# Masking the scores of both half-heads with one VectorE instruction over two PSUM banks

## The chip, the cores and the metric

The kernel runs on one core of one Trainium2 chip. The metric is the device time of one execution in microseconds (us), taken on that core; lower is better. Three runs of the kernel before lie between 1209.99 and 1215.49 us, with a median of 1213.58 us.

## The reference, cut to what matters

A linear attention with a decay per channel feeds two mixtures of experts. The change lies in the attention alone.

```python
# attention: 4 batches x 8 heads, 768 steps, 48 channels
for t in range(S):
    state = alpha[:, :, t, :, None] * state + einsum('bhd,bhe->bhde', k[:, :, t], v[:, :, t])
    y[:, :, t] = einsum('bhd,bhde->bhe', q[:, :, t], state)
x = y.transpose(0, 2, 1, 3).reshape(3072, 384)
# mixture 1: each row goes to the best of 8 experts, out = gate * (relu(x @ w1[e]) @ w2[e])
# mixture 2: out = sum over 4 experts of p[:, e] * (relu(x @ w1[e]) @ w2[e])
```

## The kernel before, in words

The 3072 rows are cut into 24 units of 128 steps, six for each batch. Eight heads are held as four pairs, and the two heads of a pair lie on partitions 0 to 47 and 64 to 111 of the same tiles: these are the two halves, `h` = 0 and 1.

One pass of the loop at L819 works on several units at once, in an order written out by hand (the schedule is manual, so each engine runs its instructions in program order):

- `prep1` (VectorE, two scans per piece, L434 and L446) forms the running products of the decay for a coming group of three units; `prep2` (GpSimd, L459 and L460) multiplies them into the queries and keys.
- `S1(u)` multiplies keys with queries into scores. Eight matmuls (L480), in the order pair 0 half 0, pair 0 half 1, pair 1 half 0 and so on, write two PSUM tiles `A0` and `A1` of one bank (512 fp32 columns) each, one for each half. Then two VectorE instructions (L485), 512 columns each, multiply the tiles with the causal mask `tri` (128 columns, repeated four times) into the SBUF tile `At`. The rest of `S1` transposes the keys (`kn`, L492).
- `S3(u-2)` transposes the finished outputs of an earlier unit (`fin`, L558); `S2(u-1)` multiplies the masked scores of the unit before with the values (`y`, L516), adds the part of the state (L525) and forms the update of the state (`U`, L537), which VectorE adds at L547 to L550.

The matmuls of L480 appear in the trace as two passes each, so 16 for a unit. The masks of a unit thus stand in VectorE's queue between the scans of `prep1` and the state update, and the next unit's score matmuls may overwrite a bank only after its mask has been read.

The pool `psA` (two banks, tag "A") hands its banks out in turn. It also serves what comes after the attention: `early_rows` and `early_g1` (tiles `ext` and `eh`, the first 224 rows of the first expert, L686 to L711), the transposes `xt0` and the tiles `h` of the first expert (L159, L160). At the second expert the pools are closed (L247) and others take the eight banks. From there on come the experts: matmuls L135 to L137, L233 to L235 and L301 to L303, with a ReLU split by ScalarE (L126) and VectorE (L127).

Of the kernel before, what the change touches and what calls it, by code (L numbers as in the profile page):

```python
# [7 lines left out]
F32 = mybir.dt.float32  # L8
# [5 lines left out]
ALU = mybir.AluOpType  # L14
AX = mybir.AxisListType
PSUM = bass.MemoryType.PSUM

B, H, S, D = 4, 8, 768, 48
# [20 lines left out]
@with_exitstack  # L39
def tile_main(ctx: ExitStack, tc: tile.TileContext, a: dict, out: bass.AP):  # L40
    nc = tc.nc

    const = ctx.enter_context(tc.tile_pool(name="const", bufs=1))
    small = ctx.enter_context(tc.tile_pool(name="small", bufs=2))
    dram = ctx.enter_context(tc.tile_pool(name="dram", bufs=1, space=bass.MemoryType.DRAM))

    xs = dram.tile([E1 * NR, DM], F32, name="xs")
    info_d = dram.tile([NT, 8], F32, name="info_d")


    units = [(0, e, f) for e in range(E1) for f in range(NFB)]
    units += [(1, e, f) for e in range(E2) for f in range(NFB)]
    wraw, wtile, ids = {}, {}, {}
    w_loaded, w_split = [0], [0]

    def load_w(n):
        while w_loaded[0] < min(n, len(units)):
            u = w_loaded[0]
            t = wst.tile([128, 2 * DM], F32, tag="wraw", name="wraw")
            src = a["wu"][u]  # L60
            if NFB <= u < E1 * NFB:
                e = a["wu"][0:E1 * NFB].rearrange("(e f) r c -> e f r c", f=NFB)
                src = e[bass.ds(ids[u // NFB], 1), u % NFB].rearrange("o r c -> (o r) c")
            nc.sync.dma_start(out=t, in_=src)
            wraw[u] = t
            w_loaded[0] += 1

    def split_w(n):
        while w_split[0] < min(n, len(units)):
            u = w_split[0]  # L70
            load_w(u + 1)
            r = wraw.pop(u)
            t = wun.tile([128, 2, 2 * DM], F32R, tag="wu", name="wu")
            nc.scalar.activation(out=t[:, 0], in_=r, func=AF.Copy)  # L74
            nc.gpsimd.tensor_tensor(out=t[:, 1], in0=r, in1=t[:, 0].bitcast(F32), op=ALU.subtract)  # L75
            wtile[u] = t
            w_split[0] += 1

    with tc.manual_schedule():
        ti = const.tile([128, 2, 128], F32, name="ti")  # L80
        ident = ti[:, 1]
        inf = const.tile([128, 24, 8], F32, name="inf")
        keep = {
            "ident": ident,
            "ti": ti,
            "ordi": const.tile([128, 8], I32, name="ordi"),
            "offi": const.tile([128, 8], I32, name="offi"),
            "posi": const.tile([128, 24], I32, name="posi"),
            "inf": inf,
            "flag": const.tile([1, 1], I32, name="flag"),  # L90
            "ft": const.tile([128, 3], F32, name="ft"),
            "ones": const.tile([128, 8], F32, name="ones"),
        }
        with ExitStack() as fast:
            wun = fast.enter_context(tc.tile_pool(name="wun", bufs=10))
            wst = fast.enter_context(tc.tile_pool(name="wst", bufs=3))
            banks = fast.enter_context(ExitStack())
            ps = (banks.enter_context(tc.tile_pool(name="psA", bufs=2, space=PSUM)),
                  banks.enter_context(tc.tile_pool(name="ps1", bufs=1, space=PSUM)))
            scat = attention_and_routing(tc, a, small, keep, xs, info_d, wst, wtile, load_w, split_w, *ps)  # L100
            experts(fast, tc, a, keep, small, xs, info_d, scat, wtile, ids, load_w, split_w, out, banks, *ps)

    bad = nc.values_load(keep["flag"][0:1, 0:1], min_val=0, max_val=1000)
    with tc.If(bad > 0):
        general(tc, a, ident, out)


def order(tc, ins, names, why):
# [230 lines left out]
def attention_and_routing(tc, a, small, keep, xs, info_d, wst, wtile, load_w, split_w, psA, ps1):  # L339
    nc = tc.nc  # L340
# [4 lines left out]
    with ExitStack() as ctx:  # L345
# [14 lines left out]
        tri = keep["ti"][:, 0]  # L360
# [112 lines left out]
        def S1(u):  # L473
            g, cl = divmod(u, 3)
            At = wk.tile([128, 2, 4, 128], F32, tag="At", name="At")
            ps = [psA.tile([128, 4, 128], F32, tag="A", name=f"A{h}") for h in range(2)]
            for p in range(4):
                kt, qq = (x[g, p // 2][:, 2 * cl + p % 2, :] for x in (kts, qqs))
                for h in range(2):
                    nc.tensor.matmul(  # L480
                        ps[h][:, p, :], lhsT=kt[64 * h:64 * h + D], rhs=qq[64 * h:64 * h + D],
                        start=(p == 0), stop=True, skip_group_check=True,
                    )
            for h in range(2):
                nc.vector.tensor_tensor(  # L485
                    out=At[:, h], in0=ps[h], in1=tri.unsqueeze(1).to_broadcast([128, 4, 128]), op=ALU.mult
                )
            Ats[u] = At
            if u % 6 < 5:
                pk = ps1.tile([128, 4, R], F32, tag="kn", name="kn")  # L490
                for p in range(4):
                    nc.tensor.matmul(  # L492
                        pk[:, p, :], lhsT=kts[g, p // 2][:, 2 * cl + p % 2, :], rhs=ident[0:R, 0:R],
                        is_transpose=True, start=(p == 0), stop=True, skip_group_check=True,
                    )
                kn = wk.tile([128, 4, R], F32, tag="kn", name="kn_s")
                nc.scalar.activation(out=kn, in_=pk, func=AF.Copy)
                kns[u] = kn
# [303 lines left out]
        prep1(0, 0, 1, 3)  # L802
        prep2(0, 0, nc.vector, nc.gpsimd, 1, 3)
        S1(0)
        prep1(0, 1, 1, 3)
        prep2(0, 1, nc.vector, nc.gpsimd, 1, 3)
# [12 lines left out]
        for i in range(NU + 5):  # L819
# [26 lines left out]
            if 0 < i < NU:  # L846
                S1(i)
# [77 lines left out]
        def dot(out, t, x):  # L925
# [32 lines left out]
            out=pv, in0=ohb, in1=off.unsqueeze(1).to_broadcast([128, NU, 8]), op=ALU.mult  # L958
# [341 lines left out]
```

## Time and profile before

| | |
|---|---|
| three runs, median (lowest to highest) | 1213.58 us (1209.99 to 1215.49) |
| profiled execution, its own time | 1213.84 us |
| its span, first to last instruction | 1212.1 us |
| TensorE matmul busy | 1178.3 us, 97% of the span |
| VectorE busy | 393.9 us, 33% |
| the mask instructions (L485) | 48 of 676 ns, 30.4 us busy |
| score matmul passes (L480) | 384 in the attention, up to 146 us |
| mean granted TensorE clock | 0.987 of full speed |

The profile lists, for one execution, what each engine did and what it waited for. TensorE's busy share is high all the way through, and VectorE's is high in the first tenth of the span alone, so the share over the whole span says little about a stage: the stretch that holds the changed instructions is the attention, the first 164 us, and it has to be read by itself.

### The profile page before, as it was taken

Reading aid. Unit: us, or ns where it says so; the run is one execution under the profiler, and the core shown is the slowest. Engines: PE = TensorE matmul, PEld = TensorE weight load, DVE = VectorE, ACT = ScalarE, POOL = GpSimd, SP = SyncE. Lnnn points to the kernel's source line nnn. Section 1 sums busy time; section 2 is a strip of 40 time slices with the busy share of each in tenths; the row PEclk is TensorE's granted clock in tenths of the full one; section 3 lists DMA queues with packets and bytes.
Section 4 is the critical chain, followed back from the end, with each engine's and each line's share of the span. In section 5 each row is a group of like instructions: output and inputs, shape, how many; then the busy total and the mean of one; then the engine's idle time right before and its main releaser. Section 6 shows DMA issues by size and latency. Waiting matters only on the chain.

```text
span 1212.1 us, 17429 instructions
## 1 busy us (share of the span) xinstructions
PE 1178.3 (97%) x7219; PEld 1080.6 (89%) x7219; DVE 393.9 (33%) x823; ACT 326.6 (27%) x640; POOL 307.1 (25%) x221
## 2 busy tenths in 40 slices
PE   5999999999999999999999999999999999999996
PEld 4888889999999999999999999999999999999996
DVE  8999653222222222222221222222222212222221
ACT  2466524444444211111311111221111131111111
POOL 3558724776676200000400000220000030111111
PEclk9999979999999999999999999999999999999998
DMA  9995235554434200000300000120000010000000
GB/s 229 275 284 184 93 114 157 151 146 136 141 118 120 67 1 1 1 1 1 92 14 1 1 1 1 40 66 1 1 1 1 1 40 1 27 27 27 27 27 29
DMA packets 30032, 79.98 MB, mean 66 GB/s; under 512 B 7352, under 2 KB 11064, under 8 KB 28376
## 3 DMA queue, kind: packets, MB, share of 16 engines
q1 hardware_dynamic: 26104, 69.25, 19.7%
q0 software_dynamic: 3840, 9.54, 2.2%
q8 instruction: 58, 0.95, 0.3%
q14 instruction: 30, 0.25, 0.1%
HBM read 65.21 MB, written 13.57 MB: 65 GB/s over the span
## 4 chain that ended last, share of the span: by engine, by line
PE 86%; DVE 5%; issue 3%; POOL 0%; ACT 0%; DVEq 0%; POOLq 0%; ACTq 0%
PE h L135 14%; PE h L137 13%; PE h L136 13%; PE p L303 11%; PE p L302 11%; PE p L301 11%; PE o L234 3%; PE o L235 3%; PE o L233 3%; DVE bf L446 1%; DVE At L485 1%; PE fin L558 1%; PE y L516 1%; DVE G L434 1%; PE A L480 1%
## 5 line engine op out<-in xcount | busy, mean ns | idle before, releaser
L127 DVE SCALAR_TENSOR_TENSOR hl<-h,hh 128x512 fp32r<-128x512 f32 (+9 forms) x264 | 169.9, 644 | 733.4 <-ACT hh L126 719.0
L126 ACT ACTIVATE hh<-h 128x512 fp32r<-128x512 f32 (+9 forms) x264 | 148.3, 562 | 726.2 <-PE h L137 724.5
L75 POOL TENSOR_TENSOR wu<-wraw,wu 128x768 fp32r<-128x768 f32 x96 | 176.5, 1842 | 650.4 <-ACT wu L74 650.4
L303 PE MATMUL p<-wu,hl 128*128 128x384 f32 x768 | 258.8, 337 | 0.0
L302 PE MATMUL p<-wu,hh 128*128 128x384 f32 x768 | 258.2, 336 | 0.0
L301 PE MATMUL p<-wu,hh 128*128 128x384 f32 x768 | 258.0, 336 | 0.0
L135 PE MATMUL h<-x,wu 128*128 128x512 f32 (+1 forms) x600 | 233.0, 388 | 0.0
L137 PE MATMUL h<-x,wu 128*128 128x512 f32 (+1 forms) x600 | 230.6, 384 | 0.0
L136 PE MATMUL h<-x,wu 128*128 128x512 f32 (+1 forms) x600 | 227.9, 380 | 0.0
L302 PEld LDWEIGHTS p<-wu,hh 128*128 128x128 f32 x768 | 144.3, 188 | 7.4
L301 PEld LDWEIGHTS p<-wu,hh 128*128 128x128 f32 x768 | 144.4, 188 | 7.1
L303 PEld LDWEIGHTS p<-wu,hl 128*128 128x128 f32 x768 | 144.3, 188 | 0.0
L137 PEld LDWEIGHTS h<-x,wu 128*128 128x128 f32 x600 | 112.6, 188 | 26.6
L136 PEld LDWEIGHTS h<-x,wu 128*128 128x128 f32 x600 | 112.8, 188 | 16.1
L135 PEld LDWEIGHTS h<-x,wu 128*128 128x128 f32 x600 | 112.8, 188 | 14.5
L74 ACT ACTIVATE wu<-wraw 128x768 fp32r<-128x768 f32 x96 | 80.3, 840 | 44.2 <-PE p L303 34.1
L314 POOL DMA_INDIRECT out_dram<-acc,toki x24 | 23.4, 975 | 183.3 <-DVE acc L310 178.5
L135 PE MATMUL h<-xh,wu 128*128 128x224 f32 (+7 forms) x192 | 67.4, 351 | 0.3 <-DVE xl L198 0.3
L234 PE MATMUL o<-hl,wu 128*128 128x224 f32 (+7 forms) x192 | 65.6, 342 | 0.1
L233 PE MATMUL o<-hh,wu 128*128 128x224 f32 (+7 forms) x192 | 65.6, 342 | 0.0
L137 PE MATMUL h<-xl,wu 128*128 128x224 f32 (+7 forms) x192 | 65.5, 341 | 0.0
L136 PE MATMUL h<-xh,wu 128*128 128x224 f32 (+7 forms) x192 | 65.5, 341 | 0.0
(164 smaller groups left out, 1089.1 us busy)
## 6 DMA issues: line engine op xcount, KB each, us to landing
wraw<-in_wu_dram SPq DMA_DIRECT2D x96, 384.0 KB
tin<-in_aqk_dram SPq DMA_DIRECT2D x14, 1011.1 KB
xw<-xs SPq DMA_DIRECT2D x7, 672.0 KB
v<-in_v_dram SPq DMA_DIRECT2D x8, 576.0 KB
xs<-pre SPq DMA_DIRECT2D x8, 480.0 KB
tin<-in_aqk_dram SPq DMA_DIRECT2D x2, 448.0 KB
tin<-in_aqk_dram SPq DMA_DIRECT2D x2, 225.8 KB
tin<-in_aqk_dram SPq DMA_DIRECT2D x2, 224.0 KB
```

The source lines that it names most:

```text
L74: nc.scalar.activation(out=t[:, 0], in_=r, func=AF.Copy)
L75: nc.gpsimd.tensor_tensor(out=t[:, 1], in0=r, in1=t[:, 0].bitcast(F32), op=ALU.subtract)
L126: nc.scalar.activation(out=hh[:, 0:n], in_=ps, func=AF.Relu)
L127: nc.vector.scalar_tensor_tensor(out=hl[:, 0:n], in0=ps, scalar=0.0, in1=hh[:, 0:n].bitcast(F32), op0=ALU.max, op1=ALU.subtract)
L135: nc.tensor.matmul(ps, lhsT=w[:, 0, ks], rhs=xh(k), start=(k == 0), stop=False)
L136: nc.tensor.matmul(ps, lhsT=w[:, 1, ks], rhs=xh(k), start=False, stop=False)
L137: nc.tensor.matmul(ps, lhsT=w[:, 0, ks], rhs=xl(k), start=False, stop=(k == KD - 1))
L233: nc.tensor.matmul(o, lhsT=w[:, 0, ds], rhs=hh[:, 0:n], start=(f == 0), stop=False)
L234: nc.tensor.matmul(o, lhsT=w[:, 0, ds], rhs=hl[:, 0:n], start=False, stop=False)
L301: nc.tensor.matmul(o, lhsT=hh[:, js], rhs=w[:, 0, DM:2 * DM], start=(f == 0), stop=False)
L302: nc.tensor.matmul(o, lhsT=hh[:, js], rhs=w[:, 1, DM:2 * DM], start=False, stop=False)
L303: nc.tensor.matmul(o, lhsT=hl[:, js], rhs=w[:, 0, DM:2 * DM], start=False, stop=(f == NFB - 1))
```

## The change

The two score tiles of a unit become one tile of two banks, `[128, 2, 512]`, which is allocated once for the whole run by a small class `Banks`. The score matmuls write slices of it; one VectorE instruction of 1024 columns, with the mask repeated eight times, reads both banks and writes the whole of `At`. All other users of `psA` call `Banks.tile`, which hands out the two banks of the same tile in turn.

```diff
-            ps = (banks.enter_context(tc.tile_pool(name="psA", bufs=2, space=PSUM)),
+            ps = (Banks(banks.enter_context(tc.tile_pool(name="psA", bufs=1, space=PSUM))),
                   banks.enter_context(tc.tile_pool(name="ps1", bufs=1, space=PSUM)))
...
+class Banks:
+    def __init__(self, pool):
+        self.both = pool.tile([128, 2, 512], F32, name="A")
+        self.n = 0
+
+    def tile(self, shape, *_, **__):
+        self.n += 1
+        return self.both[0:shape[0], self.n % 2, 0:shape[1]]
...
         def S1(u):
-            ps = [psA.tile([128, 4, 128], F32, tag="A", name=f"A{h}") for h in range(2)]
+            ps = psA.both.rearrange("p h (a c) -> p h a c", a=4)
             for p in range(4):
                 kt, qq = (x[g, p // 2][:, 2 * cl + p % 2, :] for x in (kts, qqs))
                 for h in range(2):
                     nc.tensor.matmul(
-                        ps[h][:, p, :], lhsT=kt[64 * h:64 * h + D], rhs=qq[64 * h:64 * h + D],
+                        ps[:, h, p, :], lhsT=kt[64 * h:64 * h + D], rhs=qq[64 * h:64 * h + D],
                         start=(p == 0), stop=True, skip_group_check=True,
                     )
-            for h in range(2):
-                nc.vector.tensor_tensor(
-                    out=At[:, h], in0=ps[h], in1=tri.unsqueeze(1).to_broadcast([128, 4, 128]), op=ALU.mult
-                )
+            nc.vector.tensor_tensor(
+                out=At.rearrange("p h a c -> p (h a) c"), in0=ps.rearrange("p h a c -> p (h a) c"),
+                in1=tri.unsqueeze(1).to_broadcast([128, 8, 128]), op=ALU.mult,
+            )
```

## Rows read from the trace of the kernel before

**Rows 1.** The page's chain that ended last: shares by engine, then by line.
```profile
PE 86%; DVE 5%; issue 3%; POOL 0%; ACT 0%; DVEq 0%; POOLq 0%; ACTq 0%
```
**Rows 2.** Busy time by stretch: length, PE, PEld, DVE, ACT, POOL; PEclk, DMA, GB/s.
```profile
20.00:113.00 93.00, 88.28 (x1117) 77.14 (x1113) 85.11 (x198) 51.34 (x141) 57.87 (x42) 0.98 0.92 268
113.00:137.00 24.00, 23.89 (x312) 21.12 (x314) 16.86 (x41) 15.87 (x42) 17.75 (x14) 0.93 0.26 92
187.00:1212.00 1025.00, 1013.46 (x5326) 935.12 (x5324) 244.99 (x408) 234.19 (x394) 205.67 (x134) 1.00 0.14 42
```
**Rows 3.** VectorE groups by line from 20 to 113 us: busy, mean ns, idle before.
```profile
L485 DVE TENSOR_TENSOR At<-A,ti 128x512 f32<-128x512 f32 x32 | 20.2, 672 | 0.0
```
**Rows 4.** The chain in order of time: start us, us, what.
```profile
58.71 1.16 PE A L480 x14
...
92.16 1.16 PE A L480 x14
...
113.58 1.16 PE A L480 x14
...
136.43 1.27 DVE At L485 x2
...
146.05 1.27 DVE At L485 x2
```
**Rows 5.** VectorE in order of time: start, us, line, op, tiles, count, idle before.
```profile
51.24 1.26 DVE L485 TENSOR_TENSOR At<-A,ti 128x512 f32<-128x512 f32 x2
52.51 0.06 DVE L431 MEMSET dcon<- 112x3 f32 x1
...
99.32 1.26 DVE L485 TENSOR_TENSOR At<-A,ti 128x512 f32<-128x512 f32 x2
...
99.90 0.68 DVE L485 TENSOR_TENSOR At<-A,ti 128x512 f32<-128x512 f32 x1
100.59 0.06 DVE L431 MEMSET dcon<- 112x3 f32 x1
```
**Rows 6.** First and last of the 16 pairs from 20 to 113 us, same columns.
```profile
23.02 1.26 DVE L485 TENSOR_TENSOR At<-A,ti 128x512 f32<-128x512 f32 x2
...
112.26 1.26 DVE L485 TENSOR_TENSOR At<-A,ti 128x512 f32<-128x512 f32 x2
```
**Rows 7.** VectorE groups, shapes apart: busy us, mean ns, idle before.
```profile
L485 DVE TENSOR_TENSOR At<-A,ti 128x512 f32<-128x512 f32 x48 | 30.4, 676 | 2.3 <-PE A L480 1.6 <-PE kn L492 0.7
...
L198 DVE TENSOR_TENSOR xl<-xt,xh 128x448 fp32r<-128x448 f32 x3 | 1.9, 625 | 3.6 <-ACT xh L197 3.6
...
L198 DVE TENSOR_TENSOR xl<-xt,xh 128x224 fp32r<-128x224 f32 x3 | 1.1, 388 | 2.9 <-ACT xh L197 2.9
```
**Rows 8.** Who waited for whom: VectorE from 126 to 168 us, then TensorE's from 50 to 113.
```profile
DVE At L485 <- PE A L480: 1.6, 3, 1.1
...
PE A L480 <- DVE At L485: 2.9, 4, 1.0
PEld A L480 <- DVE At L485: 6.0, 9, 1.4
```
**Rows 9.** TensorE in order of time, around 58 us and around 88 us.
```profile
58.12 1.75 PE L480 MATMUL A<-bf,G 48*128 48x128 f32 x16 [0.95 <-DVE At L485]
59.80 0.60 PE L492 MATMUL kn<-ti,G 112*128 112x112 f32 x4
60.24 1.83 PE L558 MATMUL fin<-cst,yt 112*128 112x104 f32 x8
62.00 1.91 PE L516 MATMUL y<-At,v 128*64 128x128 f32 x16
...
87.53 1.05 PE L558 MATMUL fin<-cst,yt 112*128 112x104 f32 x8
88.52 1.09 PE L516 MATMUL y<-At,v 128*64 128x128 f32 x16
```
**Rows 10.** Busy by stretches of 4 us, TensorE alone: length, PE; PEclk, DMA, GB/s.
```profile
56.00:60.00 4.00, 2.94 (x38) 1.00 1.12 369
60.00:64.00 4.00, 4.00 (x39) 0.57 0.97 293
```
**Rows 11.** All engines in order of time after the attention: a later user of the banks.
```profile
170.40 0.61 DVE L711 SCALAR_TENSOR_TENSOR eh<-eh 128x448 fp32r<-128x448 f32 x1
170.68 2.55 PE L724 MATMUL eo<-eh,wu 128*128 128x224 f32 x18
170.87 0.55 ACT L710 ACTIVATE eh<-eh 128x448 fp32r<-128x448 f32 x1 [2.08 <-PE eh L702]
```

## The prediction

> **What bounds the kernel now.** I read the chain that ended last first: 86% of it is TensorE and 5% VectorE [rows 1]. So the kernel as a whole is bound by matmuls, and a VectorE edit can only pay in the stretches where the chain runs through VectorE. The busy times by stretch say where those are [rows 2]. From 20 to 113 us VectorE is busy for 85.11 of 93 us, and nearly nothing keeps it idle: the attention's scans and masks set the pace there. From 113 to 137 us it is busy for 16.86 of 24 us and TensorE for 23.89: the pace has passed to TensorE. From 187 us to the end TensorE is busy for 1013.46 of 1025 us, and the masks are long over. What the change does to the first 164 us is therefore handed on to the end microsecond for microsecond, and nothing else of it counts.
>
> Next the groups by line. In the VectorE-bound stretch 32 mask instructions take 20.2 us, with no idle time before them [rows 3]; they are 16 pairs [rows 6], one for each unit. That is the whole sum at stake: 16 pairs of 24. Of the other eight, one comes before 20 us, where VectorE soon stands waiting for loaded data, and seven come after 113 us, where VectorE has slack.
>
> **The change, part by part.** *Two instructions of 512 columns become one of 1024.* A mask lasts 0.676 us [rows 7], but a pair doesn't last 1.35 us: it takes 1.26 us from its first start to its last end, and the next instruction stands 1.27 us after the first start [rows 5]. The second mask starts 0.58 us after the first (99.90 against 99.32 us). The two already overlap by 0.1 us. What is left to gain is small. The price of a column comes from the tensor_tensor at L198, which reads PSUM as the mask does: 625 ns at 448 columns and 388 at 224 [rows 7], so 237 / 224 = 1.06 ns a column. 512 columns more cost 0.54 us, and the new instruction 0.676 + 0.54 = 1.22 us. Against 1.26 that saves 0.04 us a pair, and 16 x 0.04 = 0.7 us on VectorE's part of the chain.
>
> No row shows an instruction of over 512 columns out of PSUM, nor one that runs across the edge of two banks, so I bound it from both sides. At least it is 1024 columns with no fixed part, 1.08 us, which saves 0.18 us a pair or 2.9 us in all. At most, if nothing is shared, it is two single masks, 1.35 us, which loses 0.09 us a pair or 1.5 us. I take 1.22, since it lies on the line through three measured sizes.
>
> The Trainium skill speaks for more. "VectorE: DVE Perf Modes", section "The DRAIN you can't avoid", says that an operation doesn't start until the pipe of the one before is empty, and advises fewer operations; by it each instruction taken out would give back its whole fixed part. The trace doesn't agree: the second mask starts 0.1 us before the first one's end [rows 5]. What that rule would give stands below as a rival.
>
> *The score matmuls lose their early start.* Before, the first half's bank is free when the first mask ends, while the second mask still runs. TensorE used that: at 58.12 us two of the 16 passes of L480 ran ahead, and the other 14 followed from 58.71 us, when the second mask was done [rows 4, 9]. Now all 16 wait for the end of the one mask. The first two passes then stand in line behind it: 14 passes take 1.16 us [rows 4], so two take 0.17. Queued behind the waiting matmuls on TensorE are the key transposes, `fin` and `y` of the earlier units. TensorE waits for the mask at L480 often between 50 and 113 us (4 matmul and 9 weight-load waits [rows 8]), but mostly VectorE is still busy with scans when the scores arrive, and the delay is covered by them; without that cover each place would cost the same 0.17 us. On the chain the step appears three times, at 58.71, 92.16 and 113.58 us [rows 4]: 3 x 0.17 = 0.5 us. The mask's own gain of 0.04 at these places is in the sum already.
>
> *The mask waits for all eight matmuls, not for seven.* Where VectorE waits for the scores, the mask starts one matmul later (two passes, 0.15 us) and lasts 0.04 us less: some 0.1 us each. VectorE waits for the scores three times after 126 us, 1.6 us in all [rows 8], and the chain goes through the masks at 136.43 and 146.05 us [rows 4]: 2 x 0.1 = 0.2 us. Behind the mask on VectorE stand the routing steps and the state update; `y` of this unit needs `At` only one pass of the loop later, so the later end of its first half costs nothing (cover: a whole unit's matmuls, over 4 us).
>
> *The shared tile.* The two banks stay two, and the later users still take them in turn, so the same reader must be done before the same writer starts. I cost it at nothing; the rival below tells what it costs if the sharing makes one bank wait for the other.
>
> **The sum.** -0.7 + 0.5 + 0.2 = 0.0 us. The profiled execution took 1213.84 us (span 1212.1 and 1.7 us around it) and would take about the same; it lies 0.26 us above the median of the runs, so in terms of that median I forecast 1213.5 us.
>
> **The rivals.** *First, the fixed part is paid in full for each instruction.* It is 0.676 - 0.54 = 0.14 us. If the records' starts are stamped early and hide it, the fusion gives 16 x 0.14 = 2.2 us, less the 0.7 us above: 1212 us, and 1211.3 at the lower bound of 2.9 us. For it speaks that mask records start before their predecessor has ended; against it, that the next instruction follows the pair after 1.27 us, which has no room for it [rows 5].
>
> *Second, slower: a read over two banks runs at half the rate.* The place is the mask itself; the price is 0.14 + 1024 x 2.1 ns = 2.3 us instead of 1.26, so 1.04 us a pair, and 16 x 1.04 = 17 us: 1230 us. It decides from a third of that rate loss on (0.38 us a pair gives 6.1 us). Nothing in the trace speaks for it; no row excludes it.
>
> *Third, slower: the lost early start costs clock.* Before the passes at 58.12 us TensorE stood idle for 0.95 us, and after them its granted clock fell: 0.57 on average from 60 to 64 us, so mostly the lower level of 1.2 GHz, after a stretch with 2.94 us busy of 4 [rows 10]. There `fin` took 1.83 us and `y` 1.91, against 1.05 and 1.09 at 88 us [rows 9]: 1.6 us for one such episode. With the early start gone that idle time grows to some 1.4 us without a break, and more episodes may follow. VectorE's pace hides most of them; each that the chain meets costs 1.6 us. Two give 1217 us; from four on (6.4 us, 1220) it is a loss of over 0.5%. The skill speaks for the early start: "PSUM — Partial Sum Buffer", section "Summary: rules for kernel authors", has a matmul write another bank than the one being read, which one read of both banks rules out. The trace agrees that the early start was used, for two passes at 58.12 us.
>
> *Fourth, it isn't only the mask that changes.* If waits are kept for the whole shared tile, the four `eh` steps after the attention must wait for each other's readers: 0.55 us of ScalarE and 0.61 of VectorE each [rows 11]. Of four such waits, about 1.2 us each, the matmuls of L724 (2.55 us) cover some [rows 11]; with three open it is 3.5 us: 1217 us.
>
> **How the numbers follow.** I give the forecast 0.80, the full fixed part 0.07, the half rate 0.03, the clock 0.06 and the whole-tile waits 0.04. The range: the bounds of the mask give -2.9 + 0.7 and +1.5 + 0.7 us around 1213.5, so 1211.3 to 1215.7. The runs themselves lie up to 3.6 us below and 1.9 us above their median; I allow 2.4 us on either side for that, and come to 1209 to 1218. It holds two clock episodes, the whole-tile waits and the full fixed part too; the half rate and four episodes are outside. A measurement of this kernel can tell about 0.5%, 6.1 us, from no change. Slower by more: the half rate 0.03, half of the clock's 0.06, and 0.01 of the waits, 0.07. Faster by more: no mechanism here reaches 6 us alone; 0.03 of the forecast's share, in case existing low-clock stretches (some 1.6 us each) fall away. Within: 0.90.
>
> **What would show it.** Right: 24 mask instructions of about 1.22 us, followed at once by their successor; score passes that run 16 in a row after the mask, with no two ahead; VectorE's part from 20 to 113 us shorter by under 1 us; the expert stages unchanged. Wrong: a mask of 1.08 us or less, or of 1.35 or more; new low-clock stretches in the first 164 us; new waits of `eh` or `h` for the other bank's readers between 160 and 205 us.

## The result, and the profile after

The changed kernel takes 1220.94 us (median of seven runs, 1216.27 to 1225.66) against 1214.72 us for the kernel before beside it: 6.2 us apart. The measured ratio is 1.0067, 95% interval 1.0046 to 1.0088: some 8 us slower, with 5.6 to 10.7 us as the interval. A later set of runs on another occasion gave 1.0081 (1.0062 to 1.0100). The forecast was no change, 1213.5 us, with a range up to 1218; it was wrong.

The profiled execution took 1216.27 us, its span is 1214.5 us. I read it in the order of the prediction. First the mask, which answers to [rows 5] and [rows 7]; these are VectorE's rows of the kernel after (L496 is the mask, L443 the memset behind it), then its group over the attention:

```profile
48.43 1.20 DVE L496 TENSOR_TENSOR At<-A,ti 128x1024 f32<-128x1024 f32 x1
49.64 0.06 DVE L443 MEMSET dcon<- 112x3 f32 x1
...
L496 DVE TENSOR_TENSOR At<-A,ti 128x1024 f32<-128x1024 f32 x24 | 28.9, 1203 | 2.3 <-PE A L492 2.3
```

One mask of 1024 columns takes 1.20 us, and its successor starts 1.21 us after it, against 1.27 for the pair before. So 0.06 us a unit are saved, and a read across the edge of two PSUM banks costs nothing extra that can be seen: 512 columns more cost 1197 - 672 = 525 ns (both are means from 20 to 113 us, of 16 masks after and of the 32 of [rows 3]), 1.03 ns a column, against 1.06 at L198 within one bank. The mask did what was forecast, and the score passes run 16 in a row, as the prediction's signs had it.

Next the busy times by stretch (columns as in [rows 2]); the last line is from the kernel before, for the stretch above it:

```profile
20.00:113.00 93.00, 84.17 (x1157) 74.19 (x1155) 87.23 (x192) 54.64 (x147) 58.24 (x42) 0.98 0.87 265
113.00:137.00 24.00, 22.62 (x316) 20.10 (x316) 15.94 (x41) 14.90 (x40) 20.09 (x15) 0.93 0.27 92
164.00:187.00 23.00, 18.43 (x145) 17.33 (x146) 12.99 (x46) 6.07 (x14) 5.56 (x4) 0.93 0.49 155
```

```profile
164.00:187.00 23.00, 22.20 (x170) 21.66 (x170) 12.70 (x57) 6.05 (x14) 7.35 (x6) 0.88 0.46 139
```

The attention isn't slower: the last mask starts at 143.4 us, 2.6 us earlier than before (146.0). That is one execution of each, and 1.8 us of it are there already at the third mask (31.0 against 32.8 us), so it is no gain of the change. The surprise is from 164 to 187 us, where TensorE is busy for only 18.43 of 23 us, against 22.20 before. That is the stage after the last mask: the early rows and the start of the first expert. Its waits say why. These are TensorE's waits between 150 and 230 us, in the kernel after (L204 is `xt`, L147 the first `h` matmuls, L698 `ext`, L714 `eh`; all four are written to the shared tile, which the trace calls `A`; `eo` isn't):

```profile
PE A L204 <- DVE xl L210: 1.7, 2, 0.9
PE A L698 <- DVE ext L688: 1.4, 1, 1.4
PE A L147 <- DVE xl L210: 0.9, 1, 0.9
PE A L147 <- DVE hl L139: 0.9, 1, 0.9
...
PE A L714 <- ACT eh L722: 0.7, 1, 0.7
...
PE eo L736 <- DVE eh L723: 0.6, 1, 0.6
PE A L714 <- DVE ext L688: 0.6, 1, 0.6
```

These are eight waits, 6.8 us in all. The last two, 1.2 us, are not for a bank: `eo` and `eh` wait there for the data that they multiply, as they do in the second profile of before (0.5 and 0.6). The six others, 5.6 us, are waits for readers of the tile. In the kernel before the same view has 0.7 us at `xt`, 0.3 at `h` and 0.2 at `eh`; its second profile, below, has 2.1 us there (0.7 at `xt`, 0.6 at `eh`, 0.5 at `eo`, 0.3 at `h`); the 0.3 at `h` is at the second expert, where after has it too. In order of time the three transposes of the first expert look like this after:

```profile
179.62 0.36 PE L204 MATMUL A<-ti,xw 112*128 112x112 f32 x2
180.02 0.36 ACT L209 ACTIVATE xh<-A 128x224 fp32r<-128x224 f32 x1 [1.88 <-PE A L204]
180.41 0.39 DVE L210 TENSOR_TENSOR xl<-A,xh 128x224 fp32r<-128x224 f32 x1 [0.95 <-ACT xh L209]
180.86 0.41 PE L204 MATMUL A<-ti,xw 112*128 112x112 f32 x2 [0.87 <-DVE xl L210]
...
182.14 0.41 PE L204 MATMUL A<-ti,xw 112*128 112x112 f32 x2 [0.87 <-DVE xl L210]
...
183.43 0.37 PE L147 MATMUL A<-xh,wu 128*128 128x224 f32 x1 [0.87 <-DVE xl L210]
...
186.30 0.55 PE L147 MATMUL A<-xh,wu 128*128 128x224 f32 x1 [0.87 <-DVE hl L139]
```

Each step writes one bank of the tile, then ScalarE and VectorE read it, and only after both have read does TensorE go on, though its next step writes the other bank. Transpose, read, read, transpose: the two banks work as one. The kernel before starts two transposes at once and waits only for the third (TensorE's rows of before, L192 is `xt`, L135 `h`):

```profile
183.24 0.55 PE L192 MATMUL xt<-ti,xw 112*128 112x112 f32 x4
184.47 0.41 PE L192 MATMUL xt<-ti,xw 112*128 112x112 f32 x2 [0.68 <-DVE xl L198]
184.76 0.37 PE L135 MATMUL h<-xh,wu 128*128 128x224 f32 x1
```

### The profile page after: what moved, and what is told of

It is laid out like the page before. It is cut to its first block, busy times and chain, and to the rows that moved or that the text cites. A ratio compares the mean times of both kernels' runs of the same rounds, so it can differ in the third digit from the quotient of the medians.

```text
span 1214.5 us, 17409 instructions
## 1 busy us (share of the span) xinstructions
PE 1170.6 (96%) x7219; PEld 1074.2 (88%) x7219; DVE 393.4 (32%) x799; ACT 326.8 (27%) x640; POOL 306.8 (25%) x221
## 4 chain that ended last, share of the span: by engine, by line
PE 85%; DVE 9%; issue 3%; DMA 1%; POOL 1%; ACT 1%; SPq 0%; DVEq 0%; POOLq 0%; ACTq 0%
PE h L147 13%; PE h L149 13%; PE h L148 13%; PE p L315 11%; PE p L314 11%; PE p L313 11%; PE o L246 3%; PE o L247 3%; PE o L245 3%; DVE bf L458 2%; DVE G L446 2%; DVE At L496 2%; PE A L714 1%; PE eo L736 1%; PE xt L204 1%
## 5 line engine op out<-in xcount | busy, mean ns | idle before, releaser
L139 DVE SCALAR_TENSOR_TENSOR hl<-h,hh 128x512 fp32r<-128x512 f32 (+8 forms) x256 | 166.7, 651 | 726.0 <-ACT hh L138 726.0
L138 ACT ACTIVATE hh<-h 128x512 fp32r<-128x512 f32 (+8 forms) x256 | 145.2, 567 | 720.4 <-PE h L149 720.4
L147 PE MATMUL h<-x,wu 128*128 128x512 f32 (+1 forms) x600 | 233.0, 388 | 0.0
L313 PEld LDWEIGHTS p<-wu,hh 128*128 128x128 f32 x768 | 144.4, 188 | 7.1
L147 PEld LDWEIGHTS h<-x,wu 128*128 128x128 f32 x600 | 112.8, 188 | 14.5
L245 PE MATMUL o<-hh,wu 128*128 128x224 f32 (+7 forms) x192 | 66.0, 344 | 0.0
L247 PE MATMUL o<-hh,wu 128*128 128x224 f32 (+7 forms) x192 | 65.8, 343 | 0.0
L147 PE MATMUL h<-xh,wu 128*128 128x448 f32 (+6 forms) x168 | 60.6, 360 | 0.3 <-DVE xl L210 0.3
L148 PE MATMUL h<-xh,wu 128*128 128x448 f32 (+6 forms) x168 | 58.9, 350 | 0.0
## 6 DMA issues: line engine op xcount, KB each, us to landing
tin<-in_aqk_dram SPq DMA_DIRECT2D x14, 1011.1 KB, 10.6
```

The costliest lines, as they stand in the source:

```text
L138: nc.scalar.activation(out=hh[:, 0:n], in_=ps, func=AF.Relu)
L139: nc.vector.scalar_tensor_tensor(out=hl[:, 0:n], in0=ps, scalar=0.0, in1=hh[:, 0:n].bitcast(F32), op0=ALU.max, op1=ALU.subtract)
L147: nc.tensor.matmul(ps, lhsT=w[:, 0, ks], rhs=xh(k), start=(k == 0), stop=False)
L148: nc.tensor.matmul(ps, lhsT=w[:, 1, ks], rhs=xh(k), start=False, stop=False)
L245: nc.tensor.matmul(o, lhsT=w[:, 0, ds], rhs=hh[:, 0:n], start=(f == 0), stop=False)
L247: nc.tensor.matmul(o, lhsT=w[:, 1, ds], rhs=hh[:, 0:n], start=False, stop=(f == NFB - 1))
```

## The experiments

The theory (W in the expectations): the program waits for the whole shared tile, not for a bank of it, wherever the tile's other users take the banks in turn; the time is lost after the attention. The rival (M): the fused mask itself costs it, by the score matmuls' lost early start and the clock behind that.

To set the executions beside each other I cut each profile at three starts in the order of time: the last mask, the first `ext` matmul and the first `o` matmul of the first expert. From the last mask to `ext` it takes 12.6 to 12.9 us in most kernels (12.9 us in the second profile of before; the first has 15.4, and e3b and e4c 13.9), so three columns are enough. All in us, the last column to about 0.1:

| kernel | banks of early rows / first expert | last mask starts | `ext` to first `o` | first `o` to end of span |
|---|---|---|---|---|
| before, two profiles | own / own | 146.0, 149.5 | 25.5, 25.3 | 1025.1, 1025.1 |
| e6 (two masks, no early start) | own / own | 145.6 | 25.1 | 1025.1 |
| e1 (one mask) | own / own | 144.4 | 25.3 | 1026.0 |
| e7 (one mask, same places) | own / own | 144.9 | 25.5 | 1026.5 |
| e4, three profiles (one mask) | shared / own | 145.2, 148.1, 146.9 | 27.1, 29.5, 27.7 | 1026.0, 1026.1, 1026.0 |
| e3, two profiles (one mask) | own / shared | 152.0, 146.9 | 30.7, 30.8 | 1026.6, 1026.5 |
| after, three profiles (one mask) | shared / shared | 143.4, 152.9, 147.1 | 32.1, 35.9, 31.7 | 1026.1, 1025.7, 1026.1 |
| e2 (two masks) | shared / shared | 150.0 | 31.9 | 1026.3 |

**e1_own_banks: the change without sharing after the attention.** The score tile of two banks has a pool of its own, which is closed ahead of the early rows; then two single banks are handed out in turn, as before.

```diff
-            ps = (Banks(banks.enter_context(tc.tile_pool(name="psA", bufs=1, space=PSUM))),
-                  banks.enter_context(tc.tile_pool(name="ps1", bufs=1, space=PSUM)))
+            ps1 = banks.enter_context(tc.tile_pool(name="ps1", bufs=1, space=PSUM))
+            ps = (Banks(tc, banks), ps1)
...
+    def split(self):
+        self.stack.close()
+        self.both = None
+        self.pool = self.banks.enter_context(self.tc.tile_pool(name="psA2", bufs=2, space=PSUM))
...
                     if r > last:
+                        psA.split()
                         early_rows()
```

> The one mask of 1024 columns stays, on one score tile of two banks; ahead of the early rows that tile's pool is closed and two banks of their own are handed out in turn, as in the kernel before. Theory W (waits between the two banks of the shared tile, after the scores are done, cost the time): TensorE's waits for ScalarE and VectorE at ext, eh, xt and h fall from 6.8 us in the profile of after to some 1.2 as before, the low clock from 183 to 190 us goes too, and the time is 1213 to 1216 us, a ratio to the kernel before of 0.998 to 1.001. Theory M (the fused mask itself, with the lost early start of the score passes and the clock behind it): nothing of that changes, so the time stays at that of after, 1219 to 1222 us, a ratio of 1.004 to 1.007.

Measured: 1212.96 us against 1211.21, ratio 1.0015 (0.9995 to 1.0035). The ratio lies a little over the expected 0.998 to 1.001, which the interval takes in, and the whole interval lies under the 1.004 of M. From `ext` to the first `o` it takes 25.3 us, as before, and the waits at `eh`, `eo` and `xt` are 1.6 us in all. TensorE's order of time at the same place in e1 (L213 is `xt`, L156 `h`):

```profile
178.60 0.55 PE L213 MATMUL xt<-ti,xw 112*128 112x112 f32 x4
...
179.83 0.41 PE L213 MATMUL xt<-ti,xw 112*128 112x112 f32 x2 [0.68 <-DVE xl L219]
...
180.13 0.37 PE L156 MATMUL h<-xh,wu 128*128 128x224 f32 x1
```

Two transposes start together again, the third waits 0.68 us, and `h` starts 1.5 us after the first `xt`, not 3.8. W holds, and M falls: the fused mask is still in, and nearly all of the loss is gone.

**e2_two_masks: the shared tile with the old masks.**

```diff
-            nc.vector.tensor_tensor(
-                out=At.rearrange("p h a c -> p (h a) c"), in0=ps.rearrange("p h a c -> p (h a) c"),
-                in1=tri.unsqueeze(1).to_broadcast([128, 8, 128]), op=ALU.mult,
-            )
+            for h in range(2):
+                nc.vector.tensor_tensor(
+                    out=At[:, h], in0=ps[:, h], in1=tri.unsqueeze(1).to_broadcast([128, 4, 128]), op=ALU.mult
+                )
```

> The opposite half: the shared tile of two banks for all users as in after, but the mask in two instructions of 512 columns each, as before. Theory W: the waits at ext, eh, xt and h stay, and the mask's own gain of 16 x 0.06 us is lost: 1220 to 1223 us, a ratio to before of 1.005 to 1.008. Theory M: back to the kernel before, 1213 to 1216 us, a ratio of 0.998 to 1.001.

Measured: 1220.32 us, ratio 1.0079 (1.0052 to 1.0106), with the same waits as after (from 187 us, L204 and L147):

```profile
187.38 0.41 PE L204 MATMUL A<-ti,xw 112*128 112x112 f32 x2 [0.87 <-DVE xl L210]
188.67 0.41 PE L204 MATMUL A<-ti,xw 112*128 112x112 f32 x2 [0.87 <-DVE xl L210]
189.95 0.37 PE L147 MATMUL A<-xh,wu 128*128 128x224 f32 x1 [0.87 <-DVE xl L210]
```

The whole loss is there without the fused mask. e2 doesn't bring back the early start: its score matmuls, too, wait for both masks (8.5 us up to 230 us, against 4.1 before), since they write the shared tile. So e2 takes out the fused mask alone, e1 keeps both parts of M and loses little, and e6 below has the lost early start by itself. W and M are told apart by e1 and e2 together.

**e4_split_late and e3_shared_expert: which of the two users.** e4 calls `psA.split()` at the start of the first expert, so the early rows share and the first expert doesn't. e3 splits as e1 does and joins the banks again there:

```diff
+        psA.join()
         window(0)
         place(1)
```

> As e1, but the shared tile is given up later: the early rows (ext, eh) still use it, the first expert (xt, h) has two banks of its own. It divides theory W's cost. If the first expert's waits and the low clock behind them are the larger part (2.8 us of waits and some 3.3 of clock against 3.1 for the early rows): 1216 to 1218 us, a ratio of 1.001 to 1.003. If the early rows are the larger part: 1218 to 1221 us, 1.004 or more. Theory M: as after, 1219 to 1222 us.

> The counterpart of e4_split_late: one mask of 1024 columns; the early rows (ext, eh) have two banks of their own, and the first expert (xt, h) uses one shared tile of two banks again. Read from the profiles (from the first ext to the first o matmul: 25.3 us in e1, 27.1 in e4, 32.1 in after) the first expert's sharing costs 5.0 us and the early rows' 1.8: then this run takes a ratio to before of 1.0055, some 1218 us. Read from the timed medians (1.0015, 1.0063, 1.0067) it is the other way round: the early rows' sharing costs nearly all and this run takes about 1.002, some 1214 us. In the trace, in both cases, xt and h wait for VectorE at each step (1.7 us at xt, 1.8 at h).

Measured: e4 1217.51 us, ratio 1.0063 (1.0041 to 1.0085); e3 1221.56 us, ratio 1.0074 (1.0048 to 1.0101). So each alone loses. The expectation from the profiles was right for e3 (1.0055 is within the interval), and the other one, that the early rows' share is nearly all, is out. e4's own ratio fell where its expectation had put the early rows as the larger part (1.004 or more), which e3 contradicts. By e4's median the early rows cost more than its first profile shows. Two further runs were to settle that, one of them timed:

> e4_split_late once more, for a second profile, since the first fell on its fastest run. If the early rows' sharing costs clock in most executions, TensorE's clock from the last score mask to 175 us is below that of the first profile (0.83 from 137 to 164 us, 0.98 from 164 to 187), and from ext to the first o matmul it takes 29 to 32 us. If not, 27 us again.

> e4_split_late again, timed beside the changed kernel on one chip. Its profiles from ext to the first o matmul (27.1 and 29.5 us against 25.3) account for 2 to 4 us over e1, its median for 5.8. If the median was right: 1.005 to 1.007 again. If the profiles are: 1.002 to 1.004.

e4b took 1218.14 us and has 29.5 us from `ext` to the first `o`; its clock from 164 to 187 us is below that of e4's first profile, while from 137 to 164 us it is above it (0.92 against 0.83). These are the stretch of e4, then of e4b (length, PE, PEclk, DMA, GB/s):

```profile
164.00:187.00 23.00, 20.88 (x173) 0.98 0.51 161
```

```profile
164.00:187.00 23.00, 21.12 (x150) 0.79 0.41 138
```

e4c, timed, gave 1216.29 us, ratio 1.0040 (1.0023 to 1.0057), with 27.7 us in that stretch; its interval takes in both expectations. I take 2 to 4 us for the early rows (27.1, 27.7 and 29.5 against 25.3); the longer times go with the lower clocks from 164 to 187 us (0.98, 0.89 and 0.79). e4's first ratio, 5.8 us over that of e1, would ask for some 2 us more, and that stays unexplained. The ratios of e3 and e4 can't simply be added either: over e1 they are 7.1 and 5.8 us, and after, which shares both, is 6.3 or 8.0 us over it in its two sets. For the second profile of e3:

> e3_shared_expert once more for a second profile. The first took 30.7 us from ext to the first o matmul, 5.4 over e1, and its last score mask came at 152 us, 6 to 8 us later than in the others. If the first expert's waits are the cause and the late mask was of that execution: 30 to 32 us again, with the mask between 143 and 153 us.

It has 30.8 us from `ext` to the first `o` (first profile 30.7) and its last mask at 146.9 us, so the late mask of the first was of that execution, as expected.

**e6_no_early_start: the lost early start by itself.** The kernel before, with its own banks and two masks, and one wait more:

```diff
+                    if p == h == 0 and masks:
+                        order(tc, ins, masks[-1:], "both masks of the unit before")
```

> The kernel before with one wait more: the first score matmul of a unit waits for both masks of the unit before, not for the first alone; pools and masks are those of before. It measures the lost early start of the score passes by itself. If it is worth what the prediction put it at (0.5 us at three places): no difference, a ratio of 0.999 to 1.002, and TensorE's waits for the mask at the score matmuls grow from 4.1 us to 5 or 6. If it costs the clock too (a low-clock stretch of 1.6 us each): 1.003 or more. It also says why e1 isn't faster than before, though each of its masks takes 0.06 us less: by the lost early start (then this run is slower by 1 to 2 us), or by nothing that can be measured.

Measured: 1212.21 us against 1212.20, ratio 1.0008 (0.9991 to 1.0024). TensorE's waits for the mask at the score matmuls, in e6 over the first 230 us, against 4.1 us before:

```profile
PE A L481 <- DVE At L488: 8.9, 7, 1.8
```

They more than double, and nothing can be measured of it; the prediction's cover, VectorE being the slower one there, is the likely reason. The kernel after has 8.7 us in the same place. The expectation of 5 or 6 us for the waits was too low, that of the time held.

**e7_same_places: what is left in e1.** e1 isn't faster than before, though its masks are. One of its waits is new, at the second expert (waits of TensorE in e1 from 181 to 300 us):

```profile
PE h L156 <- DVE x L241: 1.2, 1, 1.2
```

e7 takes the later pools in another order, so that this tile falls on another bank:

```diff
-                psx = c1.enter_context(tc.tile_pool(name="psx", bufs=2, space=PSUM, reuse_waits="tile"))
                 psh = c1.enter_context(tc.tile_pool(name="psh", bufs=3, space=PSUM, reuse_waits="tile"))
                 pso = c1.enter_context(tc.tile_pool(name="pso", bufs=1, space=PSUM, reuse_waits="tile"))
+                psx = c1.enter_context(tc.tile_pool(name="psx", bufs=2, space=PSUM, reuse_waits="tile"))
```

> As e1_own_banks, with the pools of the later experts taken in another order, so that each of their tiles follows the same earlier tile as in the kernel before. In e1 the first h of the second expert waits 1.2 us for a VectorE step of the first expert's output, which before doesn't do, and from the first o matmul to the end it takes 1026.0 us against 1025.1. Expected: that wait is gone, 1025.1 us again, and the ratio to before is that of e1 less 0.0008, 1.0007, so with the mask's own gain of 1.0 us the time lies between 1 us under and 2 us over the kernel before. If it is 1.002 or more, something in the attention with the fused mask costs 2 us or more that I haven't named.

Measured: 1213.93 us against 1211.25, ratio 1.0024 (1.0008 to 1.0041): over the expected 1.0007. The wait at the second expert is gone, but from the first `o` to the end it takes 1026.5 us, not 1025.1. The loss moved: the transposes of all experts start at the same distance from the first `o` as before (179.3 us for the last), and the first `p` matmul of the second mixture comes 218.65 us after it, against 217.24 before. There the pools change once more, and now the first `h` of the second mixture falls on a bank that is still read (TensorE in order of time, e7, then the same wait in e1 at the second expert):

```profile
397.66 0.50 PE L156 MATMUL h<-x,wu 128*128 128x512 f32 x1 [1.18 <-DVE x L241]
```

```profile
199.39 0.47 PE L156 MATMUL h<-xh,wu 128*128 128x448 f32 x1 [1.17 <-DVE x L241]
```

With the 1.4 us and no gain from the masks the sum is 1.0012, inside the interval; whether the attention with the fused mask costs something more, as the expectation put it for 1.002 and over, these runs leave open. No version beat the kernel before, and the 1.0 us of the masks is too little for these runs to show.

**Second profiles of both kernels.**

> The kernel before, unchanged, for a second profile. In the first, 15.4 us passed from the last mask to the first ext matmul, against 12.7 in after, e1, e2 and e4, with VectorE waiting 3.4 us and TensorE's queue standing still at 150 to 153 us. If that stall belongs to the kernel, it is there again; if it was of that execution alone, 12.7 us, and the first profile of before was some 2.7 us slower than it need be.

> The changed kernel once more, unchanged, for a second profile: the first one was of its fastest run. Theory W: the same waits at ext, eh, xt and h, 6 to 7 us in all, and a stretch of low clock at the first expert; the score stage ends within 3 us of where it did. Theory M: the difference to the first profile lies in the score stage, in stretches of low clock before 150 us.

> The changed kernel again, timed on the same chip as e7 and e4c. By the parts read from the profiles (6.7 to 10 us from ext to the first o matmul, 1.0 us after it, less 1.0 us of the masks) it is 6.7 to 10 us over the kernel before: a ratio of 1.0055 to 1.008. Its profile shows 31 to 36 us from ext to the first o matmul, with the waits of xt, h, ext and eh in it.

The kernel before took 1214.64 us and 12.9 us from the last mask to `ext`: the stall of 2.5 us in its first profile was of that execution. The kernel after took 1229.11 us in its second profile, 8 us above most of its runs, and 1219.82 us in the timed set (1.0081). All three of its profiles have the same eight waits. The one of 1229.11 us has them in a lower clock as well (TensorE from 164 to 187 us):

```profile
164.00:187.00 23.00, 19.07 (x113) 0.70 0.23 80
```

against 0.93 in the first and 0.95 in the third, and its third mask comes at 37.0 us (31.0 to 35.1 in the other kernels and profiles), where VectorE still waits for loaded data. Its last mask starts at 152.9 us, 9.4 us later than in the first profile, so the expectation of 3 us missed: most of what it takes over the first lies ahead of the last mask, 6.0 us of it ahead of the third. The rest, 3.4 us from the third mask to the last, lies within what other executions show there, with two masks too (111.4 to 117.4 us over all profiles).

## Why the prediction was wrong, point by point

**What bounds the kernel: right, but read too narrowly.** I wrote that what the change does to the first 164 us is handed on to the end, "and nothing else of it counts". The attention does behave so. But the change also touched the banks of the stage from 155 to 190 us, and I left that stage out of the sum because no mask lies in it.

**The mask: right.** 1.22 us forecast, 1.20 measured; 0.04 us a unit forecast, 0.06 measured; 0.7 us in all forecast, and 16 x 0.06 = 1.0 worked out from the measured ones. The rule of the Trainium skill ("VectorE: DVE Perf Modes", "The DRAIN you can't avoid"), by which the full fixed part would have come back, doesn't hold here: 0.06 us came back, not 0.14. I had left out that the same section makes an exception: an operation that isn't held starts earlier. (The advice to have fewer operations stands on that page, but under "Rules for kernel authors".) The trace is like the exception: the second mask starts 0.58 us after the first, which lasts 0.68.

**The lost early start: it is lost, and its price can't be seen.** Forecast 0.5 us at three places. e6 has 1.0008 (0.9991 to 1.0024), which neither shows the 0.5 us nor excludes them. The 0.2 us for masks that start a matmul later can't be seen either: VectorE's idle time before the masks is 2.3 us after, and 1.6 + 0.7 = 2.3 us before [rows 7].

**The sum for the attention, 0.0 us: in keeping with the profiles.** The last mask starts at 147.8 us on the mean of the four profiles with two masks, and at 147.2 on that of the ten with one, with a spread of 143 to 153 between executions. From the third mask to the last it takes 114.1 and 113.2 us on the same means. It cannot be told from nothing.

**The shared tile, costed at nothing: this is the step that failed.** I wrote that "the same reader must be done before the same writer starts". In the program that was built, any reader of the tile must be done before any writer of it starts. The mechanism stood among the rivals, as the fourth, but it was mis-sized twice. I gave it 0.04, and I priced it at 3.5 us, at `eh` alone. The first expert, which I had named in the kernel's description as a user of the same pool, wasn't in the price at all, and there the loss is larger: 30.7 and 30.8 us against 25.3 (e3 against e1), 5.4 us and more. The early rows cost 2 to 4 us, near my 3.5, but by luck: I had priced three waits of 1.2 us at `eh`, and the bank waits that came are one of 1.4 us at `ext` and one of 0.7 at `eh`, with a lower clock in some executions. Both together are 6.8 and 6.4 us in two profiles of after (32.1 and 31.7 against 25.3) and 10.6 in the one with the low clock.

How the 5.4 us come about can be read in the profiles. Before, `xt` to `h` takes 1.5 us; shared, 3.8 us, since each transpose waits for two readers. `h` to the first `o` takes 2.2 us before, 5.2 in e3 and 4.9 after: 0.9 us of it is the wait for `hl`, and the rest goes with the clock. TensorE's granted clock after from 183 to 191 us and in e1 from 180 to 188, the eight microseconds from the first `h` on, in which after gets through 33 matmuls and e1 through 67:

```profile
183.00:191.00 8.00, 6.70 (x33) 0.57 0.59 184
```

```profile
180.00:188.00 8.00, 7.85 (x67) 1.00 0.64 190
```

The three waits of 0.87 us up to the first `h`, with 0.4 us of transposes between them, are followed by some seven microseconds mostly at the lower level of 1.2 GHz, in which an `h` matmul takes 0.21 us from start to start and not 0.11. It is so in all six profiles with a shared first expert: over the eight microseconds from the first `h` their granted clock is 0.57 to 0.60, and in the eight with own banks there it is 1.00. The rest of the low stretch falls behind the first `o` and makes the 1.0 us by which 1026.1 exceeds 1025.1 in after.

**The parts add up for the first set, not quite for the second.** 6.4 to 6.8 us from `ext` to the first `o`, 1.0 behind it and -1.0 from the masks are 6.4 to 6.8 us, a ratio of 1.0053 to 1.0056; the measured ones are 1.0067 (1.0046 to 1.0088) and 1.0081 (1.0062 to 1.0100). The second asks for some 3 us more by its ratio and 2 by its medians (8.6 us apart), and its interval leaves the sum out. Low-clock executions like that of 1229.11 us (10.6 us in place of 6.4) may supply it; that is argued, not shown.

**The other rivals.** The half rate across two banks is out (1.20 us). The clock rival had the kind of loss right, idle time with the lower clock behind it, but the wrong place: it came at the first expert. At the score matmuls e6 shows no loss; its interval would still hold one episode of 1.6 us, but not two.

## What to carry to other kernels

When buffers that were separate become slices of one tile, list every user of the old buffers and ask of each whether its next write may now have to wait for a reader of the other slice; double buffering is lost wherever the program's waits are kept per tile. Give the fused tile a lifetime of its own and let the other users have separate tiles again (e1), and check which bank each later tile falls on, since even the order of the pools is worth a microsecond (e1, e7). A gain of 0.06 us in 16 places is less than two of the waits of 0.87 us that it brought.

## What the runs showed that I had not expected

A VectorE instruction that reads 1024 columns across two PSUM banks pays no more for a further column than one that stays within a bank: 525 ns for the second 512 columns, 1.03 ns each, against 1.06 at L198. TensorE's waits for the mask can grow from 4.1 to 8.9 us without a measurable change of the time. And the start of the run differs by several microseconds from one execution to the next: the third mask starts between 31.0 and 37.0 us in the three profiles of the same changed kernel.
